# Merging the two halves of each expert chunk into one PSUM bank and one operation, and a reworked weight preparation and load order, in a top-k attention and two-expert kernel

## The chip, the cores and the metric

The kernel runs on one core of a Trainium2 chip. The metric is the device time of one execution in microseconds (us). The five engines are PE (TensorE, with its weight loads shown apart as PEld), DVE (VectorE), ACT (ScalarE), POOL (GpSimd) and SP (SyncE, which here issues every transfer).

## The reference

```python
def _attn_ref(q, k, v):                      # 4 batches, 8 heads, 576 positions, 64 wide
    scores = scale * np.matmul(q, k.transpose(0, 1, 3, 2))
    kth = np.partition(scores, -32, axis=-1)[..., -32:-31]
    scores = np.where(scores >= kth, scores, -1000000000.0)
    scores = scores - np.max(scores, axis=-1, keepdims=True)
    attn = np.exp(scores)
    attn = attn / (np.sum(attn, axis=-1, keepdims=True) + 1e-09)
    return np.matmul(attn, v)

def _moe_ref(x, w_in, w_out):                # 2304 tokens, 512 -> 2048 -> 512
    h = np.maximum(x @ w_in, 0.0)
    return h * h @ w_out

def _moe2_ref(x, w1, w2, w3, w_out):         # 512 -> 768 -> 512
    h = np.maximum(np.maximum(x @ w1, x @ w2), x @ w3)
    return h @ w_out
```

The result is `_moe2_ref(_moe_ref(attention))`, with the attention output laid out as 2304 tokens of 512. Everything is float32 on the outside.

## The kernel before

**Work.** There are 20 attention tiles (four of 128 rows and one of 64 in each of 4 batches), each with 8 heads, and nine expert blocks of 256 tokens, each fed by two or three of the tiles (`BLOCKS`).

**Attention** (`attend`). For one head of one tile PE makes 128x576 scores in two halves (L421), ACT copies them out (L447), and DVE finds the 32nd largest score by four MAX8 passes (L453) with three MATCH_REPLACE8 passes between them (L455). ACT masks and exponentiates (L310, L461, L464), POOL splits off the low half of the exponentials (L307), SP transposes them by DMA (L469), and PE multiplies by the values (L477). When the heads of a tile are done it is normalized, transposed on PE (L506) and written as a pair of float16 tiles, high and low part, into `xt` (L511, L307).

**Expert products.** A float32 product is made of three float16 products (high by high, high by low, low by high), in `group` (L645). The first expert (`moe1`) takes its 2048 hidden columns in 8 chunks of 256, each chunk in two halves of 128: 12 matmuls into one PSUM bank `b`, then ACT's relu with scale (L676), square (L678) and cast (L679), POOL's low part `hl` (L307), and then the second-stage matmuls into the bank pair `a`. A sum of squares per block (L688 on ACT, four small matmuls L694 on PE) gives the scale `ga` with which ACT and DVE write the next expert's input `yt` (L705, L707). The second expert (`moe2`) does the same with three matrices and a running maximum (L723, L726, L730), and its last products go to the output (L758, then SP).

**Weights** (`convert`). The weights come as 64-bit containers in 56 half chunks of 512 KB (L531). In each container the high 32-bit word holds sign and exponent bits to be shifted by three, and the top three bits of the low word are to be filled in below: ACT rescales the high word (L310), DVE shifts the high word left by three (L536) and the low word right by 29 (L534), and POOL adds the two into the float32 weight `w` (L538). PE takes the weights' Gram matrix (L545) for a scale. Then ACT writes the float16 high part (L572), PE makes the remainder as `di` times `w` minus the high part (L579, L580), and ACT copies that out as the low part (L582). Input weights go back to a DRAM scratch and are streamed again for every block (L636); output weights stay in SBUF as `wo` and `wo2`. Conversions of 28 chunks are spread over the first blocks by `feed`; after the second tile of the first block `feed(33)` asks for a share of the rest.

**What sets the order.** All of it is recorded as operations of a `Plan`, which runs a list scheduler over a model of costs (`run`). Each engine's queue is the order that this yields; the program at run time keeps that order and waits on semaphores. Numbers such as `WAIT`, `LW`, `rank`, `slack` and the costs (`c_act`, `c_dve`, `c_pool`, `hop`) act on nothing but the order. Buffers are counted in `nbufs`; among them two for q (`qt`), and six one-bank PSUM buffers `b`. DVE operations with `lock=True` are placed by the planner so as not to overlap POOL operations in its model.

## Time and profile before

| | |
|---|---|
| median of 3 runs | 1054.8 us (1053.51 to 1056.78) |
| profiled execution | 1051.32 us, of which the profiled span is 1049.5 us |
| PE busy | 993.9 us, 95% of the span |
| DVE busy | 847.0 us |
| ACT busy | 824.9 us |
| POOL busy | 659.8 us |
| bytes moved by DMA | 189.46 MB |

How to read it: the profile is one execution, so sums are made against its own 1051.32 us, 1.8 us of which lie outside the span. A busy share near 100% in a stretch says that the engine sets the pace there only if the others wait for it in that stretch. The stretches differ: the first 171.4 us hold attention for the first block and most of the weight preparation and no expert product, the stretch up to 900 us holds attention and expert products side by side, and the rest is expert products alone. Queues are read from rows of instructions in order of time with, in square brackets, the idle time before them and what ended it.

### The profile page before, as it was taken

What the parts mean: (1) busy time and instruction counts of PE and PEld (TensorE: products, weight loads), DVE (VectorE), ACT (ScalarE), POOL (GpSimd) and SP (SyncE); (2) the same over time, 40 slices, a digit from 0 to 9 for tenths busy, and PEclk for the clock granted to TensorE, in tenths of its full rate; (3) what the DMA queues carried; (4) which work ended last, traced back from release to release, by engine and by line L of the source; (5) the groups of instructions that cost most, each with busy time, mean ns of one, the idle gap of its engine ahead of it and who ended that gap; (6) DMA issues with size and microseconds to landing.
All of it is one profiled execution on the core that took longest, in us unless ns stands there. A gap on an engine that the chain in (4) does not pass through costs nothing.

```text
span 1049.5 us, 23814 instructions
## 1 busy us (share of the span) xinstructions
PE 993.9 (95%) x8408; PEld 793.9 (76%) x8408; DVE 847.0 (81%) x1961; ACT 824.9 (79%) x1900; POOL 659.8 (63%) x1126
## 2 busy tenths in 40 slices
PE   4868599999999999999999999999999999999998
PEld 3434346677878787889788889978887888887876
DVE  5999979999895899999999999989999996012011
ACT  4889579999988797998999789989997995452531
POOL 3678656688876566788777667887766765221211
PEclk9978659999999999999999999999999999999999
DMA  9678859988789769678866966875768669335211
GB/s 296 204 204 205 232 125 241 217 199 235 214 222 288 176 138 231 156 173 226 218 166 136 237 149 165 208 207 153 159 173 201 153 130 230 109 100 172 71 44 59
DMA packets 220536, 189.46 MB, mean 181 GB/s; under 512 B 176384, under 2 KB 185344, under 8 KB 220416
## 3 DMA queue, kind: packets, MB, share of 16 engines
q1 hardware_dynamic: 220416, 187.93, 70.3%
q8 instruction: 66, 1.08, 0.4%
q14 instruction: 54, 0.44, 0.1%
HBM read 131.79 MB, written 13.63 MB: 139 GB/s over the span
## 4 chain that ended last, share of the span: by engine, by line
PE 65%; DVE 13%; ACT 7%; DMA 6%; POOL 5%; issue 3%; SPq 0%; POOLq 0%; ACTq 0%; DVEq 0%
PE b L645 35%; PE a L645 12%; PE b L421 8%; DVE mx L453 5%; PE b L477 5%; DVE w L455 5%; PE b L579 3%; DMA wu<-in_w_dram 2%; DMA qs<-in_q_dram 1%; POOL e L307 1%; POOL hl L307 1%; DVE wu L536 1%; DMA qt<-in_q_dram 1%; PE b L545 1%; ACT e L461 1%
## 5 line engine op out<-in xcount | busy, mean ns | idle before, releaser
L453 DVE MAX8 mx<-w 128x8 f32<-128x576 f32 x432 | 315.0, 752 | 0.7
L307 POOL TENSOR_TENSOR e<-e,e 128x512 f16<-128x512 f32 (+1 forms) x288 | 210.1, 741 | 62.9 <-ACT e L464 59.4
L645 PE MATMUL b<-yt,wu 128*128 128x256 f16 x1944 | 227.0, 274 | 3.2 <-ACT r L676 1.0
L645 PE MATMUL b<-xt,wt 128*128 128x256 f16 x1728 | 220.3, 273 | 0.4 <-DVE xt L307 0.4
L645 PE MATMUL a<-hh,wo 128*128 128x256 f16 x1152 | 219.7, 273 | 0.0
L455 DVE MATCH_REPLACE8 w<-mx,w 128x576 f32<-128x576 f32 x288 | 214.1, 746 | 0.0
L645 PEld LDWEIGHTS <-wu 128*128 128x128 f16 x1944 | 186.9, 98 | 29.8 <-issue 4.1
L645 PEld LDWEIGHTS <-wo 128*128 128x128 f16 x1728 | 164.4, 98 | 25.0 <-issue 3.5
L645 PEld LDWEIGHTS <-wt 128*128 128x128 f16 x1728 | 164.7, 98 | 23.8 <-issue 3.1
L307 POOL TENSOR_TENSOR hl<-r,hh 128x256 f16<-128x256 f32 x144 | 97.3, 677 | 106.9 <-ACT hh L679 97.7
L421 PE MATMUL b<-kt,qt 128*128 128x288 f32 (+1 forms) x640 | 157.3, 372 | 6.8 <-DMA qt<-in_q_dram 3.3
L645 PE MATMUL a<-hl,wo 128*128 128x256 f16 x576 | 157.0, 273 | 0.4 <-POOL hl L307 0.4
L421 PEld LDWEIGHTS b<-kt,qt 128*128 128x128 f32 (+1 forms) x640 | 103.2, 201 | 31.8 <-issue 4.1
L310 ACT ACTIVATE e<-s,mx 128x576 f32<-128x576 f32 x144 | 112.3, 781 | 18.3 <-DVE mx L453 16.4
L447 ACT ACTIVATE s<-b 128x288 f32<-128x288 f32 x288 | 108.9, 411 | 14.1 <-PE b L421 13.5
L453 DVE MAX8 mx<-s 128x8 f32<-128x576 f32 x144 | 107.4, 752 | 12.4 <-ACT s L447 12.3
L461 ACT ACTIVATE e<-e,nb 128x576 f32<-128x576 f32 x144 | 112.3, 782 | 4.6 <-POOL nb L457 3.7
L477 PEld LDWEIGHTS <-et 128*128 128x128 f16 (+1 forms) x1440 | 84.6, 102 | 34.3 <-DMA et<-e 14.6
L455 DVE MATCH_REPLACE8 w<-mx,s 128x576 f32<-128x576 f32 x144 | 107.3, 747 | 0.0
L477 PE MATMUL b<-vt,et 128*128 128x129 f16 (+3 forms) x1440 | 93.4, 213 | 13.2 <-ACT s L447 5.2
L464 ACT CAST e<-e 128x576 f16<-128x576 f32 x144 | 97.6, 678 | 0.5
L676 ACT ACTIVATE r<-b,u 128x256 f32<-128x256 f32 x144 | 68.3, 477 | 36.7 <-PE b L645 35.8
(108 smaller groups left out, 1383.6 us busy)
## 6 DMA issues: line engine op xcount, KB each, us to landing
wu<-wsc SPq DMA_DIRECT2D x81, 512.0 KB, 4.2
wt<-wsc SPq DMA_DIRECT2D x72, 512.0 KB, 3.7
wu<-in_w_dram SPq DMA_DIRECT2D x56, 512.0 KB, 5.2
wsc<-oc SPq DMA_DIRECT2D x17, 512.0 KB, 4.8
ks<-in_k_dram SPq DMA_DIRECT2D x12, 576.0 KB, 4.7
qs<-in_q_dram SPq DMA_DIRECT2D x48, 128.0 KB, 3.5
vst<-in_v_dram SPq DMA_DIRECT2D x16, 320.0 KB, 4.3
out_dram<-ot SPq DMA_DIRECT2D x16, 256.0 KB, 2.4
```

What stands on the lines that cost most here:

```text
L307: eng.tensor_tensor(out_ap, a, b, op=ALU.subtract)
L310: return nc.scalar.activation(out_ap, src, AF.Prelu, alpha=slope, **kw)
L421: nc.tensor.matmul(ps[:, 0:HS], a, c, start=m == 0, stop=m == len(seq) - 1)
L447: act(A_S, HS, [ps], [(s, f)], lambda s=s, cs=cs, ps=ps: nc.scalar.activation(s[:, cs], ps[:, 0:HS], AF.Copy, scale=escale))
L453: dve(A_X, S, [src], [(mx, r)], lambda src=src, mx=mx, m8=m8: nc.vector.max(out=mx[:, m8], in_=src[:]))
L455: dve(A_X, S + 50, [src, (mx, r)], [w_], lambda src=src, mx=mx, m8=m8, w_=w_: nc.vector.match_replace(out=w_[:], in_to_replace=mx[:, m8], ...
L461: act(A_E, S, [e, nb], [e], lambda nb=nb, e=e: nc.scalar.activation(e[:], e[:], AF.Exp, bias=nb[:], scale=-1.0 / KEEP), psum=False, ptr=1)
L464: act(A_E, S, [e], [(e16, 0)], lambda e=e, e16=e16: nc.scalar.copy(e16[:, S:2 * S], e[:]), psum=False)
L477: nc.tensor.matmul(ps[0:n, 0:wv], et[:, mm_, c0:c1], vt[:, hh, vc, 0:wv], start=x == 0, stop=x == 8)
L579: nc.tensor.matmul(pl[:], di[:], w[:, cs], start=True, stop=False)
L645: nc.tensor.matmul(o, x, y, start=first and i == 0 and m == 0, stop=last and i == n - 1 and m == 2)
L676: act(MA, N, [ps, u1], [r], lambda r=r, ps=ps, c=c: nc.scalar.activation(r[:, 0:N], ps[:, 0:N], AF.Relu, scale=u1[:, c // 2:c // 2 + 1]), ...
```

## The change

- **Expert chunks.** The two halves of a chunk go into one bank `b` of 128x2x256 (start flag on the first half only), and each of the operations behind them (relu, square, cast, low part; copy, maximum, cast, low part; square with sum, scale, low part of `yt`) is done once over 512 columns instead of twice over 256. `DEEP`, counted in pairs now, goes from 2 to 1, and the counts of the hidden buffers are halved with the tiles twice as wide. The sum of squares needs one small matmul instead of four and one DVE reduce more.
- **Weight preparation.** POOL makes the low three bits from the top byte of the low word (multiply, add, rounded into an integer), and DVE shifts and ors in one operation with two inputs (`scalar_tensor_tensor`). POOL now stands before DVE, not behind it. Every third pair of chunks is held in a `yt` buffer.
- **Remainders of wo2.** For chunks from 25 on (the three of the last matrix) the low part is made by DVE (`DLO = 25`), not by PE and ACT. The GpSimd branch (`PLO = 28`) is never taken, since the last chunk is 27; the tiles `zg, zs, u0, fz` and the branches on `0 == 1` do nothing.
- **Loads and order.** The first k and q loads get a rank of -9; q has three buffers instead of two; the planner reckons 210 ns from a transfer's end to its reader, 1500 ns for reuse of a load's buffer, and a smaller `WAIT`, with other ranks and slacks. The output tile shares the buffers `m`.

```diff
-WAIT = 100.0
+WAIT = 30.0
+MS = 1500.0
+MD = 210.0
+MT = ('qt', 'qs', 'kt', 'ks', 'vst')
...
-                t = max(t, d.end + hop(d.eng, o.eng))
+                t = max(t, d.end + (MD if d.eng == SP else hop(d.eng, o.eng)))
...
-                        t = max(t, sorted(free[k])[u][0] + HOP)
+                        t = max(t, sorted(free[k])[u][0] + (MS if e == SP and b.tag in MT else HOP))
...
-    nbufs = {"ks": 1, "qs": 1, "vst": 1, "kt": 4, "qt": 2, "vt": 4, "sm": 2, "sc": 6, "s": 5, "w": 2, "e": 2, "e16": 3,
+    nbufs = {"ks": 1, "qs": 1, "vst": 1, "kt": 4, "qt": 3, "vt": 4, "sm": 2, "sc": 6, "s": 4, "w": 2, "e": 2, "e16": 3,
...
-             "hh": 4, "hl": 4, "h2": 6, "h3": 6, "r": 3, "m": 2, "ot": 2, ...
+             "hh": 2, "hl": 2, "h2": 3, "h3": 3, "r": 2, "m": 2, ...
...
+            if not kv:
+                plan.rank = -9.0
             if new:
                 kt = prep_k(b, p)
             qt = prep_q(b, t, p)
+            plan.rank = base
...
-                dve(C_D, 512, [hk], [hk], lambda hi=hi: nc.vector.tensor_scalar(
-                    hi().bitcast(U32), hi().bitcast(U32), 3, None, op0=SHL), rate=0.5, slack=SL / 2, lock=True)
-                dve(C_D, 512, [lk], [lk], lambda lo=lo: nc.vector.tensor_scalar(
-                    lo(), lo(), 29, None, op0=SHR), rate=0.5, slack=SL / 2, lock=True)
-                gps(C_P, 445, [hk, lk], [(w, y)], lambda w=w, cs=cs, hi=hi, lo=lo: nc.gpsimd.tensor_tensor(
-                    w[:, cs].bitcast(U32), hi().bitcast(U32), lo(), op=ALU.add))
+                top = lambda raw=raw: raw[:].rearrange("p n u -> p (n u)").bitcast(U8).rearrange("p (n u) -> p n u", u=8)[:, :, 3]
+                gps(C_P, 300, [lk], [lk], lambda lo=lo, top=top: nc.gpsimd.tensor_scalar(
+                    lo(), top(), 1.0 / 32.0, -15.5 / 32.0, op0=ALU.mult, op1=ALU.add))
+                dve(C_D, 512, [hk, lk], [(w, y)], lambda w=w, cs=cs, hi=hi, lo=lo: nc.vector.scalar_tensor_tensor(
+                    w[:, cs].bitcast(U32), hi().bitcast(U32), 3, lo(), op0=SHL, op1=OR), slack=SL / 2, lock=True)
...
+            if chunks[0] >= DLO:
+                for y in range(2):
+                    cs = slice(512 * y, 512 * y + 512)
+                    dve(C_D, 512, [w, ok, sk], [ok], lambda cs=cs, half=half, w=w: nc.vector.scalar_tensor_tensor(
+                        half(1)[:, cs], w[:, cs], sv(), half(0)[:, cs], op0=ALU.mult, op1=ALU.subtract), slack=SL / 2, lock=True)
...
         for c in range(NA):
             wk, w = stream(c, "wt")
+            ps = buf("b", [P, 2, NW])
+            r = buf("r", [P, 2, NW])
             for ff in range(2):
-                ps = buf("b", [P, 512])
-                r = buf("r", [P, NW])
-                group(ps, KD, N, lambda i, wk=wk: [wk, x], lambda kk, w=w, ff=ff: (
-                    cols(w(), 256, kk, ff), (x[:, 0, kk, 0:N], x[:, 1, kk, 0:N])), also=[r])
-                hh, hl = buf("hh", [P, NW], F16), buf("hl", [P, NW], F16)
-                act(MA, N, [ps, u1], [r], lambda r=r, ps=ps, c=c: nc.scalar.activation(
-                    r[:, 0:N], ps[:, 0:N], AF.Relu, scale=u1[:, c // 2:c // 2 + 1]), ptr=1)
...
+                group((ps, ff), KD, N, lambda i, wk=wk: [wk, x], lambda kk, w=w, ff=ff: (
+                    cols(w(), 256, kk, ff), (x[:, 0, kk, 0:N], x[:, 1, kk, 0:N])),
+                    first=ff == 0, last=ff == 1, also=[ps, r])
+            hh, hl = buf("hh", [P, 2, NW], F16), buf("hl", [P, 2, NW], F16)
+            act(MA, 2 * N, [ps, (uu, c // 2)], [r], lambda r=r, ps=ps, c=c: nc.scalar.activation(
+                r[:, :, 0:N], ps[:, :, 0:N], AF.Relu, scale=uu[:, c // 2:c // 2 + 1]), ptr=1)
+            act(MA, 2 * N, [r], [r], lambda r=r: nc.scalar.activation(r[:, :, 0:N], r[:, :, 0:N], AF.Square), psum=False)
+            act(MA, 2 * N, [r], [hh], lambda r=r, hh=hh: nc.scalar.copy(hh[:, :, 0:N], r[:, :, 0:N]), psum=False)
+            gps(A_S, 2 * N, [r, hh], [hl], lambda r=r, hh=hh, hl=hl: sub(nc.gpsimd, hl[:, :, 0:N], r[:, :, 0:N], hh[:, :, 0:N]))
...
-        pe(A_S, 812.0, [yq], [ps, ga], total)
-        dve(A_S, 1, [ps], [ga], lambda: bits(ga[:], ps[:, 0:1], EXP, EXP, AND, XOR))
+        pe(A_S, 200.0, [yq], [ps, ga], lambda: nc.tensor.matmul(ps[:, 0:2], down_t[:], yq[:], start=True, stop=True))
+        dve(A_S, 2, [ps], [ga], lambda: nc.vector.tensor_reduce(ga[:], ps[:, 0:2], op=ALU.add, axis=mybir.AxisListType.X))
+        dve(A_S, 1, [ga], [ga], lambda: bits(ga[:], ga[:], EXP, EXP, AND, XOR))
```

The start of SP's queue is the first place where the order moves. In the rows, `wu` is a half chunk of raw weights, `kt`, `qt` and `vst` are the k, q and v of the first heads; before:

```order
L849 UNCONDITIONAL_BRANCH
L531 DMA wu_124<-in_w_dram 128x1024
L531 DMA wu_132<-in_w_dram 128x1024
L531 DMA wu_134<-in_w_dram 128x1024
L531 DMA wu_136<-in_w_dram 128x1024
L531 DMA wu_138<-in_w_dram 128x1024
L358 DMA kt_140<-in_k_dram 64x1152
L358 DMA qt_143<-in_q_dram 64x256
```

And now:

```order
L548 DMA wu_128<-in_w_dram 128x1024
L548 DMA wu_136<-in_w_dram 128x1024
L548 DMA wu_138<-in_w_dram 128x1024
L368 DMA kt_140<-in_k_dram 64x1152
L368 DMA qt_142<-in_q_dram 64x256
L548 DMA wu_144<-in_w_dram 128x1024
L548 DMA wu_148<-in_w_dram 128x1024
L368 DMA vst_150<-in_v_dram 128x640
```

The first k and q stand behind three half chunks of weights, where they stood behind five.

The start of DVE's queue shows the weight preparation beside the first top-k passes; before (`s` are scores, `mx` the found maxima):

```order
L534 TENSOR_SCALAR wu_136<-wu_136 128x512
L534 TENSOR_SCALAR wu_138<-wu_138 128x512
L536 TENSOR_SCALAR wu_138<-wu_138 128x512
L453 MAX mx_210<-s_190 128x8
L455 MATCH_REPLACE w_215<-mx_210,s_190 128x576
L536 TENSOR_SCALAR wu_166<-wu_166 128x512
L453 MAX mx_210<-w_215 128x8
L534 TENSOR_SCALAR wu_166<-wu_166 128x512
```

And now, where a half chunk is one row that writes the finished weight (`wt`):

```order
L554 SCALAR_TENSOR_TENSOR wt_156<-wu_128 128x512
L554 SCALAR_TENSOR_TENSOR wt_156<-wu_136 128x512
L554 SCALAR_TENSOR_TENSOR wt_174<-wu_138 128x512
L469 MAX mx_204<-s_183 128x8
L554 SCALAR_TENSOR_TENSOR wt_174<-wu_144 128x512
L554 SCALAR_TENSOR_TENSOR wt_216<-wu_148 128x512
L471 MATCH_REPLACE w_224<-mx_204,s_183 128x576
```

Ten DVE rows of the first five half chunks became five, and the first MAX stands behind three of them. Up to the second write of the first block's `xt`, DVE's queue had 288 rows and has 240.

At the end of the last block, ACT's queue before (`r` is a hidden half, `a` the second stage's sums, `yq` their squares):

```order
L676 ACTIVATE r_16259<-b_16258,u_88 128x256
L678 ACTIVATE r_16259<-r_16259 128x256
L679 CAST hh_16288<-r_16259 128x256
L688 ACTIVATE junk,yq_16313<-a_15849 128x256 x2
L688 ACTIVATE junk,yq_16313<-a_15857 128x256 x2
```

And now:

```order
L714 ACTIVATE r_15263<-b_15262,u_88 128x512
L716 ACTIVATE r_15263<-r_15263 128x512
L717 CAST hh_15308<-r_15263 128x512
L726 ACTIVATE junk,yq_15339<-a_14949 128x512
L726 ACTIVATE junk,yq_15339<-a_14958 128x512
```

The last three operations on the hidden columns now cover the whole chunk. On PE the order of the last block is now 24 second-stage matmuls, 24 of the first stage, and so on in turn, and at the end 48 of the second stage, where it was 12 and 12 in turn with 36 at the end.

## Rows read from the trace of the kernel before

**Rows 1.** The page's part 1: busy us, share of the span, instructions.

```profile
PE 993.9 (95%) x8408; PEld 793.9 (76%) x8408; DVE 847.0 (81%) x1961; ACT 824.9 (79%) x1900; POOL 659.8 (63%) x1126
```

**Rows 2.** Busy by stretch: us and count per engine, PE clock, DMA share, GB/s.

```profile
0.00:171.40 171.40, 128.87 (x562) 72.22 (x563) 148.23 (x355) 130.73 (x250) 108.57 (x167) 0.82 0.80 215
171.40:300.00 128.60, 125.67 (x1017) 93.30 (x1015) 119.69 (x280) 117.73 (x263) 97.76 (x155) 1.00 0.83 213
300.00:900.00 600.00, 595.75 (x5617) 507.80 (x5616) 563.24 (x1291) 519.58 (x1252) 424.44 (x757) 1.00 0.77 186
900.00:1049.50 149.50, 143.61 (x1223) 120.57 (x1220) 15.86 (x38) 56.88 (x138) 29.04 (x47) 0.99 0.28 92
```

**Rows 3.** The chain that ended last, by line, of 0 to 60 and 60 to 172 us.

```profile
by line: PE b L421 20.2%; DMA qt<-in_q_dram 14.9%; DVE w L455 10.9%; DVE mx L453 10.1%; issue 7.7%; PE b L579 6.8%; DMA wu<-in_w_dram 6.1%; SPq L531 3.9%; PE b L545 3.0%; PE b L551 2.6%; DVE wu L536 2.6%; DVE wu L534 2.4%; POOL wt L538 1.7%
...
by line: PE b L421 14.8%; PE b L579 11.8%; DVE mx L453 9.6%; issue 8.6%; DVE w L455 8.5%; DMA wu<-in_w_dram 4.8%; PE b L545 4.8%; PE b L477 4.3%; DVE wu L536 4.2%; DVE wu L534 3.4%; ACT wo L572 2.9%; POOL wt L538 2.7%; PE b L580 2.5%; ACT e
```

**Rows 4.** Start of the timeline: start, us, engine, line, instructions, idle before and releaser.

```profile
0.72 2.53 SPq L531 DMA_DIRECT2D wu<-in_w_dram  x5
3.92 0.60 SPq L358 DMA_DIRECT2D qt<-in_q_dram  x1
12.99 8.01 PE L421 MATMUL b<-kt,qt 64*128 64x288 f32 x16 [3.34 <-DMA qt<-in_q_dram]
```

**Rows 5.** Busy by stretch, three stretches of 26 us in the start.

```profile
0.00:26.00 26.00, 12.41 (x45) 8.53 (x46) 14.15 (x32) 12.76 (x24) 8.88 (x22) 1.00 0.94 294
105.00:131.00 26.00, 15.17 (x79) 9.14 (x79) 26.00 (x56) 15.38 (x26) 18.03 (x26) 0.70 0.88 233
131.00:157.00 26.00, 23.69 (x72) 12.27 (x71) 19.89 (x50) 18.54 (x35) 12.82 (x24) 0.50 0.50 123
```

**Rows 6.** Groups by line and shape: busy us, mean ns, idle before and releasers.

```profile
L453 DVE MAX8 mx<-w 128x8 f32<-128x576 f32 x432 | 315.0, 752 | 0.7
L538 POOL TENSOR_TENSOR wt<-wu 128x512 uint32<-128x512 uint32 x32 | 37.6, 1188 | 18.7 <-DVE wu L534 7.5 <-DMA wu<-in_w_dram 4.1 <-PE b L579 3.6
L536 DVE TENSOR_SCALAR wu<-wu 128x512 uint32<-128x512 uint32 x56 | 30.2, 551 | 5.2 <-DMA wu<-in_w_dram 5.0
L534 DVE TENSOR_SCALAR wu<-wu 128x512 uint32<-128x512 uint32 x56 | 27.4, 493 | 4.3 <-ACT wu L310 3.8 <-issue 0.3
L500 POOL TENSOR_SCALAR xg<-xg,va 128x512 f32<-128x512 f32 x16 | 11.4, 713 | 9.3 <-DVE ia L313 6.9 <-DVE va L313 1.8 <-ACT wo L582 0.3
L307 DVE TENSOR_TENSOR xt<-b,xt 128x512 f16<-128x512 f32 x16 | 10.9, 683 | 2.7 <-ACT xt L511 2.7
```

**Rows 7.** One line's instructions: shortest, median, longest ns, first and last start.

```profile
L536 DVE TENSOR_SCALAR wu<-wu x56: 409/424/1331, 4.8 to 300.8; 128x512 uint32<-128x512 uint32 x56
```

**Rows 8.** What SP waited for, 0 to 171 us: us, times, longest.

```profile
SPq L358 <- PE b L421: 18.5, 6, 8.0
```

**Rows 9.** Timeline of PE: one pair of remainders, and the next row.

```profile
173.08 1.02 PE L579 MATMUL b<-wu,di 128*128 128x512 f32 x2
...
174.16 1.47 PE L645 MATMUL b<-xt,wt 128*128 128x256 f16 x12
```

**Rows 10.** Timeline of PE: a block's sum of squares, and the next row.

```profile
567.44 0.95 PE L694 MATMUL b<-yq,down 128*128 128x1 f32 x8
568.25 1.47 PE L645 MATMUL b<-xt,wt 128*128 128x256 f16 x12
```

**Rows 11.** Timeline of the last block: the last hidden half, and the second stage's weight loads.

```profile
1004.63 3.92 PEld L645 LDWEIGHTS <-wo 128*128 128x128 f16 x36
1005.00 0.47 ACT L676 ACTIVATE r<-b,u 128x256 f32<-128x256 f32 x1 [1.26 <-PE b L645]
1006.49 0.67 POOL L307 TENSOR_TENSOR hl<-r,hh 128x256 f16<-128x256 f32 x1 [1.95 <-issue]
```

**Rows 12.** Groups by line and shape, of operations over 512 columns on ACT and POOL.

```profile
L307 POOL TENSOR_TENSOR e<-e,e 128x512 f16<-128x512 f32 x144 | 168.8, 1173 | 62.9 <-ACT e L464 59.4 <-POOL e L307 1.2 <-ACT sc L386 0.8
L758 ACT ACTIVATE ot<-b,go 128x512 f32<-128x512 f32 x18 | 12.3, 682 | 22.1 <-PE b L645 22.0
```

More of the change, by code (lines that the diff above doesn't have):

```diff
@@ L658, in moe1 @@
         av = lambda d: pair[d // 2][:, d % 2, 0:N]
-        def stage2(f, hh, hl):
-            for d in range(KD):
-                also = [(pair[d // 2], 0)] if f in (0, 2 * NA - 1) and d % 2 else []
-                group(acc[d], 1, N, lambda i, also=also: [(wo, f // 2), hh, hl, *also], lambda i, d=d: (
-                    cols(wo[:, f // 2], DM, f % 2, d), (hh[:, 0:N], hl[:, 0:N])),
-                    first=f == 0 and d % 2 == 0, last=f == 2 * NA - 1 and d % 2 == 1)
+        uu = u0 if 0 == 1 and g == 0 else u1
@@ new lines, in stage2 @@
+        def stage2(c, hh, hl):
+            if uu is u0 and c and c % 2 == 0:
+                for pr in pair:
+                    z = slice(c // 2, c // 2 + 1)
+                    act(MA, 2 * N, [pr, (fz, c // 2)], [pr], lambda pr=pr, z=z: nc.scalar.activation(
+                        pr[:, :, 0:N], pr[:, :, 0:N], AF.Copy, scale=fz[:, z]), ptr=1)
+            for ff in range(2):
+                f = 2 * c + ff
+                for d in range(KD):
+                    also = [(pair[d // 2], 0)] if f in (0, 2 * NA - 1) and d % 2 else []
+                    group(acc[d], 1, N, lambda i, also=also: [(wo, c), hh, hl, *also], lambda i, d=d, ff=ff: (
+                        cols(wo[:, c], DM, ff, d), (hh[:, ff, 0:N], hl[:, ff, 0:N])),
+                        first=f == 0 and d % 2 == 0, last=f == 2 * NA - 1 and d % 2 == 1)
@@ L685, in moe1 @@
             stage2(*x_)
-        yq, ga, gx = buf("yq", [P, KD]), buf("ga", [P, 1]), buf("gg", [P, 1])
-        for d in range(KD):
-            act(MA, N, [pair[d // 2]], [(yq, d)], lambda d=d: nc.scalar.activation(
-                junk[:, 0:N], av(d), AF.Square, scale=2.0 ** -27, accum_out=yq[:, d:d + 1]), ptr=1)
+        yq, ga, gx = buf("yq", [P, 2]), buf("ga", [P, 1]), buf("gg", [P, 1])
+        for j, pr in enumerate(pair):
+            act(MA, 2 * N, [pr], [(yq, j)], lambda j=j, pr=pr: nc.scalar.activation(
+                junk[:, 0:2 * N].rearrange("p (a n) -> p a n", a=2), pr[:, :, 0:N], AF.Square, scale=2.0 ** -27, accum_out=yq[:, j:j + 1]), ptr=1)
@@ L690, in moe1 @@
         ps = buf("b", [P, 512])
[L692 to L696 removed]
+        ps = buf("b", [P, 512])
+        pe(A_S, 200.0, [yq], [ps, ga], lambda: nc.tensor.matmul(ps[:, 0:2], down_t[:], yq[:], start=True, stop=True))
+        dve(A_S, 2, [ps], [ga], lambda: nc.vector.tensor_reduce(ga[:], ps[:, 0:2], op=ALU.add, axis=mybir.AxisListType.X))
@@ L713, in moe2 @@
         for fp in range(NF2):
-            m = [buf("m", [P, NW]) for _ in range(2)]
+            m = buf("m", [P, 2, NW])
+            mv = lambda m=m: m[:, :, 0:N]
             kx = lambda fp=fp: u2[:, fp:fp + 1]
@@ L770 @@
         plan.rank = -1.0
-        if g == 0:
+        if g == 0 and 0 == 0:
             feed(33)
```

116 lines of the change are left out of this document (64 added, 52 removed).

## The prediction

> **What bounds the kernel now.** I read the page's busy line first [rows 1]: PE is busy 993.9 us of a span of 1049.5, DVE 847.0. An average over the span says little here, so the second view is the busy time by stretch [rows 2], and it splits the kernel in two. From 171.4 us on, where the first expert matmul starts, PE has 125.67 of 128.6, 595.75 of 600 and 143.61 of 149.5 us: 865.0 of 878.1, 13 us idle. There PE alone sets the pace; what ACT, DVE and POOL save there is worth nothing unless PE waited for it. Before 171.4 us no expert product runs, PE is busy 128.87 us at a mean granted clock of 0.82, and DVE 148.23 us. The third view is the chain that ended last in that start [rows 3]: it changes hands between PE (scores L421, remainders L579), DVE (top-k L453 and L455, and the two weight shifts L536 and L534), POOL's add L538, and transfers. So the start is a mesh in which DVE is the fullest engine but not always the last. The end is then the start's length plus PE's remaining work plus its idle time, and I price the change in these three.
>
> **1. PE's work after the start.** (a) The six wo2 remainders leave PE. One takes from 173.08 to 174.16, 1.08 us [rows 9]: 6.5 us. They were the last of 56 and lay in stretches in which PE is 98% busy. In their place DVE gets six operations of about 0.68 us (L307 on DVE [rows 6]), 4 us before DVE runs out of attention work; the last stretch of rows 2 has DVE at 15.86 of 149.5, so it is hidden by PE's expert work. (b) The sum of squares needed 8 rows of PE from 567.44 to 568.25, 0.81 us [rows 10]; one matmul of two rows leaves 0.2. Eight of nine blocks have them amid other PE work: 8 x 0.6 = 4.9 us. (c) By the order of both kernels, four score matmuls and nine value matmuls that stood ahead of the first expert matmul now stand behind it. Sixteen rows, 8 score matmuls, took 8.01 us [rows 4] at 1.2 GHz, so 0.5 us each at 2.4 GHz: 2.0, with the value ones some 2.5 us added. (d) All expert matmuls are the same in number and width. Net -8.9 us.
>
> **2. PE's idle time after the start.** Merging halves makes each operation on the hidden columns 512 wide. ACT's 512 column row is 682 ns against 470 for 256 [rows 11, 12], 0.21 more in each of three operations; POOL's is 1173 against 670, 0.50 more. That saves some 45 us of ACT over the kernel, which I count as nothing: PE's expert matmuls cover it. But the chain from the last hidden half to its low part was 1005.00 to 1007.16 [rows 11] and becomes 1.1 us longer, to 1008.3. In the order now, 24 first-stage matmuls and 24 second-stage ones lie between, at 3.92 / 36 = 0.109 us each [rows 11] 5.2 us, more than the chain of 3.7 us from 1004.63. So only the very last chunk shows: 24 second-stage matmuls cover 2.6 us, to 1007.25, and PE then waits 1.0 us for its chunk. Next, the squares, the sum and the new `yt` are two wide operations in place of four, with a reduce more: half a us either way, taken as 0. The tail after the last output matmul does not change. Net +1.0 us.
>
> **3. The start.** Three edits act on it. *First loads:* the score matmuls began at 12.99 after waiting for q, which was issued at 3.92 behind five weight loads [rows 4]. Two of these now come after it: 1.05 MB at 294 GB/s [rows 5] is 3.5 us. *DVE:* 39 half chunks stand ahead of the second `xt` write in both orders. Each cost 551 + 493 = 1.04 us [rows 6]. The new form does not occur before. The nearest row is a two-input operation over 512 columns, L307 on DVE at 683 ns [rows 6]; alone, the two old ones are 0.42 each [rows 7], so the new one saves 0.16 without contention and 0.36 if contention stays with the old. 39 x 0.36 = 14 us at best, 6 at worst short of a loss (rival E). DVE's queue also holds four MAX8 and three MATCH_REPLACE8 fewer ahead of that write, some 5 us at 752 ns [rows 6]. *POOL:* the add of 1188 ns becomes a one-input operation; the nearest row is L500's 713 ns [rows 6]. If everything on DVE counted, the start would shrink by 14 + 5 + 3.5 = 22 us. Counting what the chain held instead [rows 3]: the shifts have 5.0% of 60 us and 7.6% of 112, 11.5 us, of which a third goes, 3.8; POOL's add 4.0 us, of which 0.4 goes, 1.6; with the loads 9 us. I take 12, nearer to the chain, because DMA (0.80 of 171.4 us) and ACT (130.73) are close behind DVE in rows 2 and their work is the same. The third q buffer goes with this: SP waited 18.5 us for scores to release q, 8.0 at once [rows 8], and everything behind a waiting load on SP, weights and transposes, waited too. I give it no own price; it is what would let the 12 us come about.
>
> **Sum.** 1051.3 - 12 - 8.9 + 1.0 = 1031.4 us, 19.9 below the profiled execution. That execution is 3.5 us under the median of the runs, 1054.8, so for the median 1035 us.
>
> **The rivals.** *B, PE's clock holds.* From 105 to 157 us the granted clock was 0.70 and then 0.50 [rows 5], which is 1.2 GHz of 2.4, after a stretch in which PE was busy 15.17 of 26 us; in the second it was busy 23.69 of 26. With the higher level the same work takes half, 12 us less: 1023. For it: PE's remainders and score matmuls are spread more evenly in the new order, and the shifts that held up Gram matmuls are shorter. Against: DVE still sets the pace, so PE will still pause.
>
> *C, another engine takes over the start.* DMA needs 0.80 x 171.4 = 137 us of work and ACT 131; with queues in order and hops between, 160 us may be out of reach. Then only the loads show, or nothing: 1043.5 to 1047. For it: the shares in rows 2; against: DMA itself waited, with a share of 0.50 from 131 to 157 [rows 5].
>
> *D, no change.* The 9 us taken from PE come back as idle time, since PE's queue is in order and coarser expert operations hold banks longer, and the start stands: 1055. Against: 4 us of idle in 600 [rows 2] leave few waits to grow.
>
> *E, slower, by contention between DVE and POOL.* The shift's median is 424 ns and its longest 1331 [rows 7], 0.9 us more, as if it waited for most of one POOL operation of 1.04 to 1.19 us. The Trainium skill (SBUF — State Buffer, "Who interferes with whom") says that a DVE instruction with two SBUF inputs and a POOL instruction that reads SBUF exclude each other for the whole instruction; by that rule the new operation is exposed as the old ones were, and the longest row agrees with it. In this kernel that would mean: each new operation, 0.68 us, waits for one whole POOL operation, 1.17 [rows 12], 1.85 us against 1.04, 39 times: +31.5 us, less 5 and 3.5, +23 on the start: 1055 + 23 - 8 = 1070. It decides from 39 x (x - 1.04) = 16.4 (5, 3.5 and the 7.9 net of parts 1 and 2), a mean of x = 1.46 us per new operation. Against: the old pair, exposed twice, averaged only 0.2 us of it, and one instruction is exposed once.
>
> **Chances and range.** The forecast (1026 to 1043) 0.45, B 0.20, C 0.18, D 0.07, E 0.10. A measurement here tells some 0.3%, 3 us, from no change. A, B and C are faster, 0.83; D the same, 0.07; E slower, 0.10. The range runs from 1017, into B, to 1054, to the edge of D; beyond lie about 0.05 and 0.14.
>
> **What would show it.** Right: the first expert matmul near 159 us; first score matmul near 9.5; the new DVE operation at 0.65 to 0.8 us and POOL's at about 0.7; no remainder of wo2 on PE; PE still at 98% or more from the first expert matmul on, with about 1 us of wait before the last second-stage chunk. Wrong: the first expert matmul at 168 us or later (C, or E where the new DVE operation is above 1.3 us), or under 150 with the clock at 1.0 throughout (B), or PE idle clearly above 14 us after it (D). The largest risk is the 12 us, taken between 9 and 22, where one stall of transfers or one stretch at the lower clock is worth as much as the whole term.

## The result, and the profile after

The changed kernel takes 1025.2 us (median of 4, 1021.8 to 1027.4) against 1054.2 (1052.6 to 1056.8) of the kernel before on the same chip: a ratio of 0.972, with an interval of 0.968 to 0.976. The forecast was 1035 with a range of 1017 to 1054: the direction and the range held, and the gain is 29 us where 20 were forecast. The profiled execution took 1023.4 us, 28.0 less than before's.

The page's first part, busy time and share of each engine, answers to [rows 1]:

```profile
PE 969.9 (95%) x8336; PEld 779.5 (76%) x8336; DVE 824.0 (81%) x1848; ACT 773.5 (76%) x1570; POOL 628.6 (62%) x1027
```

PE lost 24.0 us of busy time, and the rest of its span fell from 55.6 to 51.7 us. That is the shortest account of the result: 24 us less busy, 4 us less idle. Not all of the 24 is work taken away; some 7.6 us of it are the clock, as worked out under the control for scatter below. ACT has 51 us less to do, and nothing in these two numbers needs it.

Busy time by stretch, split at the first expert matmul as in [rows 2] (us and count for PE, PEld, DVE, ACT, POOL, then PE's granted clock, DMA share, GB/s):

```profile
0.00:149.90 149.90, 117.56 (x547) 64.81 (x548) 131.70 (x301) 125.52 (x240) 94.75 (x162) 0.90 0.86 246
149.90:300.00 150.10, 142.65 (x1204) 111.87 (x1204) 143.99 (x329) 137.67 (x273) 115.98 (x181) 0.98 0.84 215
300.00:872.00 572.00, 567.81 (x5384) 484.33 (x5382) 535.20 (x1196) 467.71 (x989) 393.15 (x659) 1.00 0.77 187
872.00:1021.60 149.60, 141.90 (x1208) 118.46 (x1206) 13.06 (x24) 42.61 (x70) 24.73 (x26) 0.99 0.27 90
```

The first expert matmul comes at 149.9 us instead of 171.4, 21.6 earlier. In the start PE's idle time fell from 42.5 to 32.3 us; behind it the idle time rose from 13.1 to 19.3, and of these 6.2 us the stretch up to 300 us has 4.5. The other half of the 21.6 is PE's busy time: 547 matmuls stand ahead of the marker for 562, which is some 2 us, and the rest is the clock (0.90 for 0.82 in these rows, which leave out the first 43 us; see below).

The start of the timeline answers to [rows 4] (start, duration, engine and line, operation):

```profile
2.75 0.63 SPq L368 DMA_DIRECT2D qt<-in_q_dram  x1
3.42 1.07 SPq L548 DMA_DIRECT2D wu<-in_w_dram  x2
...
9.91 4.17 PE L431 MATMUL b<-kt,qt 64*128 64x288 f32 x8 [1.85 <-DMA qt<-in_q_dram]
```

q is issued 1.2 us earlier, two weight loads behind it, and the scores begin 3.1 us earlier, for 3.5 in the working. The new operations, by line (duration in ns as min/median/max), answer to [rows 6, 7]; first DVE's, then POOL's, then DVE's remainder of wo2:

```profile
L554 DVE SCALAR_TENSOR_TENSOR wt<-wu x24: 672/683/1052, 5.5 to 113.1; 128x512 uint32<-128x512 uint32 x24
L554 DVE SCALAR_TENSOR_TENSOR wu<-wu x24: 671/684/1031, 113.7 to 294.8; 128x512 uint32<-128x512 uint32 x24
L554 DVE SCALAR_TENSOR_TENSOR yt<-wu x8: 673/680/1242, 30.7 to 85.1; 128x512 uint32<-128x512 uint32 x8
```

```profile
L552 POOL TENSOR_SCALAR wu<-wu x56: 639/657/706, 4.8 to 292.7; 128x512 uint32<-128x512 uint8 x56
```

```profile
L592 DVE SCALAR_TENSOR_TENSOR wo<-wu,v,wo x6: 733/742/910, 165.6 to 307.9; 128x512 f16<-128x512 f32 x6
```

They cost what the nearest rows said. Contention between DVE and POOL shows little on DVE: the longest, 1242 ns, is 0.57 us over the shortest. It shows on POOL. In the timeline, one small operation on POOL undisturbed, and the same operation beside a run of five new ones on DVE (the fifth writes `yt`, from 71.80 to 72.48):

```profile
98.09 0.30 POOL L474 TENSOR_SCALAR nb<-mx 128x1 f32<-128x1 f32 x1
...
69.40 2.48 DVE L554 SCALAR_TENSOR_TENSOR wt<-wu 128x512 uint32<-128x512 uint32 x4
69.59 3.06 POOL L474 TENSOR_SCALAR nb<-mx 128x1 f32<-128x1 f32 x1 [0.85 <-DVE mx L469]
```

It ends at 72.65, behind the whole run. Against the median of their kind, fifteen POOL operations beside the new ones lost 15.2 us in all, and the new ones 1.5. In the kernel before, reckoned alike, POOL lost 11.2 us beside the two shifts and the shifts 11.0. So DVE's gain is in part contention that it no longer pays, while POOL pays more; what that costs the whole kernel no run separates.

Two views by line show what left PE. First before (busy us, mean ns of one, idle ahead), lines that were not among the rows above:

```profile
L421 PE MATMUL b<-kt,qt 128*128 128x288 f32 (+1 forms) x640 | 157.3, 372 | 6.8 <-DMA qt<-in_q_dram 3.3 <-ACT oc L582 1.5 <-ACT xs L480 1.5
...
L579 PE MATMUL b<-wu,di 128*128 128x512 f32 x48 | 25.3, 609 | 0.6 <-ACT oc L582 0.6
...
L694 PE MATMUL b<-yq,down 128*128 128x1 f32 x72 | 9.3, 245 | 0.4
L580 PE MATMUL b<-wo,nid 128*128 128x512 f16 x22 | 8.6, 391 | 0.0
```

and the same lines after:

```profile
L431 PE MATMUL b<-kt,qt 128*128 128x288 f32 (+1 forms) x640 | 148.8, 362 | 7.5 <-POOL qt L310 3.4 <-DMA qt<-in_q_dram 1.8 <-ACT xs L497 0.8
...
L605 PE MATMUL b<-wu,di 128*128 128x512 f32 x36 | 18.9, 607 | 0.2 <-POOL di L578 0.2
...
L606 PE MATMUL b<-wo,nid 128*128 128x512 f16 x16 | 6.6, 411 | 0.0
...
L731 PE MATMUL b<-yq,down 128*128 128x2 f32 x18 | 3.0, 238 | 2.3 <-ACT junk L726 2.3
```

The six remainders account for 6.4 + 2.0 = 8.4 us, the sums of squares for 6.3. The same 640 score matmuls take 8.5 us less, though nothing in them changed; the lower clock makes part of it. Matmuls of different groups overlap on PE, and a group's busy time counts the overlap too, so such differences don't add up to the 24.0 and come out larger than the time that they free.

### The profile page after: what moved, and what is told of

The parts are those of the page before. It is cut to its first block, busy times and chain, and to the rows that moved or that the text cites. A ratio compares the mean times of both kernels' runs of the same rounds, so it can differ in the third digit from the quotient of the medians.

```text
span 1021.6 us, 23034 instructions
## 1 busy us (share of the span) xinstructions
PE 969.9 (95%) x8336; PEld 779.5 (76%) x8336; DVE 824.0 (81%) x1848; ACT 773.5 (76%) x1570; POOL 628.6 (62%) x1027
## 4 chain that ended last, share of the span: by engine, by line
PE 61%; DVE 19%; ACT 7%; DMA 6%; POOL 5%; issue 3%; SPq 0%; POOLq 0%; ACTq 0%; DVEq 0%
PE b L671 34%; PE a L671 10%; DVE mx L469 9%; DVE w L471 8%; PE b L431 7%; PE b L494 4%; PE b L605 3%; DMA wsc<-oc 2%; DMA vst<-in_v_dram 1%; DMA wu<-in_w_dram 1%; POOL e L310 1%; DMA et<-e 1%; DMA qt<-in_q_dram 1%; POOL kt L310 1%; ACT e L313 1%
## 5 line engine op out<-in xcount | busy, mean ns | idle before, releaser
L469 DVE MAX8 mx<-w 128x8 f32<-128x576 f32 x432 | 311.2, 746 | 0.4
L671 PE MATMUL b<-xt,wt 128*128 128x256 f16 x1728 | 213.2, 273 | 0.0
L671 PE MATMUL a<-hh,wo 128*128 128x256 f16 x1152 | 209.8, 273 | 0.0
L431 PE MATMUL b<-kt,qt 128*128 128x288 f32 (+1 forms) x640 | 148.8, 362 | 7.5 <-POOL qt L310 3.4
L310 POOL TENSOR_TENSOR hl<-r,hh 128x512 f16<-128x512 f32 x72 | 84.5, 1174 | 88.5 <-ACT hh L717 86.5
L431 PEld LDWEIGHTS b<-kt,qt 128*128 128x128 f32 (+1 forms) x640 | 100.8, 198 | 38.2 <-issue 10.5
L313 ACT ACTIVATE e<-s,mx 128x576 f32<-128x576 f32 x144 | 112.1, 778 | 19.9 <-DVE mx L469 17.7
L463 ACT ACTIVATE s<-b 128x288 f32<-128x288 f32 x288 | 105.8, 411 | 20.4 <-PE b L431 19.4
L469 DVE MAX8 mx<-s 128x8 f32<-128x576 f32 x144 | 107.1, 746 | 6.7 <-ACT s L463 6.7
L494 PE MATMUL b<-vt,et 128*128 128x129 f16 (+3 forms) x1440 | 91.0, 212 | 3.0 <-POOL vt L310 2.8
L714 ACT ACTIVATE r<-b,u 128x512 f32<-128x512 f32 x72 | 49.6, 689 | 47.4 <-PE b L671 47.0
```

Source lines behind the costliest of these rows:

```text
L310: eng.tensor_tensor(out_ap, a, b, op=ALU.subtract)
L313: return nc.scalar.activation(out_ap, src, AF.Prelu, alpha=slope, **kw)
L431: nc.tensor.matmul(ps[:, 0:HS], a, c, start=m == 0, stop=m == len(seq) - 1)
L463: act(A_S, HS, [ps], [(s, f)], lambda s=s, cs=cs, ps=ps: nc.scalar.activation(s[:, cs], ps[:, 0:HS], AF.Copy, scale=escale))
L469: dve(A_X, S, [src], [(mx, r)], lambda src=src, mx=mx, m8=m8: nc.vector.max(out=mx[:, m8], in_=src[:]))
L494: nc.tensor.matmul(ps[0:n, 0:wv], et[:, mm_, c0:c1], vt[:, hh, vc, 0:wv], start=x == 0, stop=x == 8)
```

## The experiments

Twelve kernels ran. Theory D says that DVE's work sets the length of the start; its rival O that the order of the queues, transfers or the clock set it. Theory P says that what PE no longer does counts in full; its rival I that it comes back as idle time. For the merged halves, C, M and N are told in the expectation. Each kernel is `after` or `before` with one edit. The table has what the profiled execution of each shows: the first expert matmul, PE's busy time, how much of it lay at the lower clock (1.2 GHz; how that was counted stands with the control for scatter), and PE's idle time (span less busy); the ratio is to runs of the kernel before on the same chip.

| kernel | ratio (interval) | first expert matmul | PE busy | of it at the lower clock | PE idle |
|---|---|---|---|---|---|
| before | 1 | 171.4 | 993.9 | 79.3 | 55.6 |
| after | 0.972 (0.968 to 0.976) | 149.9 | 969.9 | 64.1 | 51.7 |
| e1_late_kq | 0.977 (0.972 to 0.982) | 154.1 | 978.0 | 85.3 | 51.8 |
| e2_two_q | 0.978 (0.972 to 0.984) | 154.3 | 974.1 | 76.1 | 58.0 |
| e3_old_prep | 0.984 (0.979 to 0.989) | 154.3 | 972.9 | 69.5 | 62.2 |
| e4_wo2_pe | 0.976 (0.971 to 0.980) | 149.8 | 975.3 | 63.0 | 51.8 |
| e5_old_plan | 0.980 (0.978 to 0.983) | 147.8 | 980.8 | 78.5 | 51.8 |
| e6_halves | 0.975 (0.971 to 0.978) | 149.7 | 973.0 | 73.1 | 50.4 |
| e7_prep_only | 1.004 (1.002 to 1.006) | 159.2 | 991.2 | 69.5 | 61.9 |
| e8_merge_twice | 1.011 (1.008 to 1.014) | 178.7 | 983.4 | 89.8 | 81.5 |
| e9_wait33 | 0.973 (0.968 to 0.977) | 154.7 | 977.4 | 80.4 | 50.8 |
| e10_plan_only | 0.993 (0.990 to 0.996) | 150.3 | 985.9 | 72.5 | 55.7 |
| e11_prep_plan | 0.987 (0.983 to 0.991) | 152.3 | 992.1 | 85.2 | 48.6 |
| e12_short_shl | 0.995 (0.992 to 0.998) | 169.4 | 992.8 | 78.7 | 52.6 |

**One part of `after` undone.** The first k and q load without their rank:

```
-            if not kv:
-                plan.rank = -9.0
```

> The changed kernel (1025.2 us) without the early rank of the first k and q loads. Theory D (DVE's work sets the length of the start, so all that delays its first MAX8 delays the end): the first score matmul moves from 9.9 back to about 13 us and the first expert matmul from 149.9 to about 153; 1028.7 us. Rival O (the start was shortened by the order of loads and buffers and by PE's clock, DVE's time is hidden): the mesh absorbs the 3 us; 1025 us.

Measured: 1029.2 us, first scores at 13.3 us. The idle time is after's; PE's busy time rose by 8, with 21 us more of it at the lower clock. The marker stands 4 us later, but the idle time ahead of it is after's too (31.8 for 32.3 us), and the interval of the ratio overlaps that of `after`: that the early loads are worth anything is not shown.

The third q buffer:

```
-"qt": 3,
+"qt": 2,
```

> The changed kernel with two q buffers instead of three. Theory D: SP waits again for scores to release q, but DVE stays the fullest engine; first expert matmul at 150 to 153 us, 1025 to 1028 us. Rival O: the wait of SP that was 18.5 us in the kernel before comes back, weights and transposes behind it are late; first expert matmul at 158 us or later, 1033 us or more.

Measured: 1030.4 us, PE idle 6.3 us more. This part works through waits, as the prediction thought, and has by the medians a price of its own of some 5 us that was put at nothing; but here too the intervals overlap.

The old weight preparation (two shifts on DVE, the add on POOL, for one DVE operation behind one on POOL) in the new kernel:

```
-                gps(..., nc.gpsimd.tensor_scalar(lo(), top(), 1.0 / 32.0, -15.5 / 32.0, op0=ALU.mult, op1=ALU.add))
-                dve(..., nc.vector.scalar_tensor_tensor(w[:, cs], hi(), 3, lo(), op0=SHL, op1=OR))
+                dve(..., nc.vector.tensor_scalar(hi(), hi(), 3, None, op0=SHL))
+                dve(..., nc.vector.tensor_scalar(lo(), lo(), 29, None, op0=SHR))
+                gps(..., nc.gpsimd.tensor_tensor(w[:, cs], hi(), lo(), op=ALU.add))
```

> The changed kernel with the weight preparation of before: two DVE shifts of some 0.5 us and POOL's add of 1.13 us in place of POOL's 0.66 us and DVE's one operation of 0.70 us. Theory D: 39 half chunks in the start cost 0.33 us of DVE each more, 13 us; first expert matmul at 163 us, 1038 us. Rival O: DVE's time is hidden; first expert matmul at 150 to 154, 1025 to 1030 us.

Measured: 1037.0 us, 12 above `after`. The time is D's, the place is not: the marker moved by 4.4 us only. The stretches:

```profile
0.00:154.30 154.30, 114.80 (x540) 63.93 (x541) 140.26 (x346) 127.20 (x244) 108.13 (x162) 0.87 0.88 239
154.30:1035.10 880.80, 858.11 (x7798) 718.59 (x7796) 692.45 (x1559) 649.10 (x1327) 541.88 (x866) 0.99 0.68 173
```

Ahead of the marker PE idled 39.5 us for 32.3, behind it 22.7 for 19.3, and it had 7 matmuls more left to do there. So a marker hides part of what a change of the start is worth; PE's idle time over the whole span shows it, +10.5. This edit gives back POOL's saving together with DVE's, so it does not tell which of the two the 12 us belong to.

The six remainders of wo2 back on PE:

```
-    DLO = 25
+    DLO = 99
-    PLO = 28
+    PLO = 99
```

> The changed kernel with the six wo2 remainders back on PE (and ACT), none on DVE. Theory P (PE sets the pace after the start, so its work counts in full): 6 x 1.08 = 6.5 us more, 1031.7 us, first expert matmul where it was. Rival I (PE's idle time after the start rose from 13 to 19 us in the changed kernel, so part of the work taken from PE came back as waits): 2 us or less, 1025 to 1027 us.

Measured: 1027.6 us, and in the profiled execution 5.5 us over after's: PE busy +5.4, idle +0.1, at the lower clock as much as in `after`. P's mechanism stands in the trace; the ratio's interval alone would not tell it from `after`.

The old numbers of the planner in the new kernel:

```
-WAIT = 30.0
+WAIT = 100.0
-    AVS = 800.0
+    AVS = 0.0
-    TA = 2.0
+    TA = 0.0
-    C0, C1 = 1.5, 0.03
+    C0, C1 = 0.5, 0.06
```

with the two terms MD and MS taken out. The early rank of the first loads, the third q buffer and everything else of `after` stay.

> The changed kernel, all its operations and buffers, ordered with the planner's numbers of the kernel before (WAIT 100, no own delays for transfers and load buffers, no slack on the value matmuls, ranks and due times as before). Theory D (DVE's and PE's saved work carries the gain): 1025 to 1031 us, first expert matmul at 150 to 156. Rival O (the order carries it): at least half of the start's 21.6 us comes back, first expert matmul at 161 us or later, 1036 us or more.

Measured: 1033.5 us, clearly above `after`, with a marker that is even earlier, 147.8. These numbers are worth 8 to 9 us, and the marker does not show it. PE's busy time is 11 us higher at an unchanged idle time, and 14 us more of it lie at the lower clock.

Separate halves in the expert stages, each half with its bank and its operations, with everything else as in `after`:

```
-            ps = buf("b", [P, 2, NW])
-            r = buf("r", [P, 2, NW])
             for ff in range(2):
+                ps = buf("b", [P, 512])
+                r = buf("r", [P, NW])
...
-    DEEP = 1
+    DEEP = 2
```

> The changed kernel with the first and second expert's chunks in halves again, one bank and one set of operations each, as before (the sum of squares and the writing of yt stay merged). Theory C (merging is hidden by PE's expert matmuls, as ACT's 45 us less were counted at nothing): within 3 us of 1025. Rival M (the longer chain of wide operations makes the 6 us of idle time that PE gained after the start): idle after the first expert matmul falls from 19 to 13 us, 1019 us. Second rival N (ACT's and DVE's saved time matters in the crowded stretch up to 300 us): 5 us or more slower, 1030 us.

Measured: 1026.3 us; idle 50.4 against 51.7. C holds: the part that gives the change its name makes no difference that can be measured, and the 38 us of ACT that it saves (811.3 for 773.5 busy) were all covered.

**More of the new operation.** `after` with each of the 56 new DVE operations issued twice in place, the order of all queues unchanged:

```
+                    for _ in range(2):
                         nc.vector.scalar_tensor_tensor(...)
```

> The changed kernel with each shift-and-or on DVE issued twice (56 more operations of 0.68 us, 39 of them in the start), with the order of all queues otherwise unchanged. Theory D: 39 x 0.68 = 27 us on the start, first expert matmul at 175 us, 1050 us. Rival O (DVE is not what the others wait for): 10 us or less, 1035 us. If DVE is the last to arrive in about half of the start, some 13 us, 1038 us.

Measured: 1066.1 us, 41 above `after`. The start (same columns as above):

```profile
0.00:178.70 178.70, 126.26 (x547) 68.90 (x548) 168.52 (x345) 127.65 (x243) 94.17 (x165) 0.85 0.75 209
```

DVE has 36.8 us more there, the marker moved by 28.8, near D's 27, and PE's idle time ahead of it rose by 20.1. Over the span DVE has 53.7 us more and PE idled 29.8 more, so more than half of the work added to DVE came through as waits of PE; most of what the 41 us hold beyond that goes with the lower clock (89.8 us of PE's busy time for 64.1). The mean of the operation rose to 0.81 to 0.87 us by tile.

**Less DVE work at an unchanged order.** `before` with the left shift on 64 of its 512 columns; all queues stay as they are:

```
-                    hi().bitcast(U32), hi().bitcast(U32), 3, None, op0=SHL)
+                    hi().bitcast(U32)[:, 0:64], hi().bitcast(U32)[:, 0:64], 3, None, op0=SHL)
```

> Before with the left shift of each prepared half chunk on 64 of its 512 columns (the other columns keep unshifted values, so the output is not the reference's); every queue has the same instructions in the same order. The shift takes some 0.1 us for 0.51, 39 of them ahead of the first expert matmul: 16 us less on DVE. Theory D (DVE sets the start's length): first expert matmul at 155 to 160 for 171.4. Rival O (order, transfers or the clock set it): within 3 us of 171.4. For the whole time: 1040 if PE keeps what the start gains, 1050 to 1055 if it is given back behind the first expert matmul, as with the new preparation alone.

Measured: 1046.9 us, marker at 169.4. The left shift is L534, the one that waits for ACT, and the right shift L536; the description of the kernel before has the two lines the other way round. The left shift took 189 ns (median) for 421, and DVE's busy time in the start fell by 8.0 us, half of what was expected; 2 us reached the marker. D fails here at the marker. What happened instead, in POOL's waits for the two shifts, first before, 0 to 171.4 us (total, times, longest):

```profile
POOL wt L538 <- DVE wu L534: 7.5, 4, 6.4
POOL wu L538 <- DVE wu L536: 5.2, 5, 2.5
POOL wt L538 <- DVE wu L536: 3.5, 4, 1.2
```

and with the short shift, 0 to 169.4 us:

```profile
POOL wt L538 <- DVE wu L534: 12.9, 4, 8.0
POOL wt L538 <- DVE wu L536: 2.3, 3, 0.9
```

The waits fell by 1 us only, 16.2 to 15.2, and those for the shorter shift grew: what is late is mostly the turn of a shift in DVE's queue, not its length. Over the span DVE has 12.3 us less, PE idled 3.0 us less, and the median is 4.8 us lower (2 to 8 by the interval). So in an order that was made for the longer work, work taken from DVE came through less than work added: a quarter of it in PE's idle time, where it was more than half in the kernel with the doubled operation.

**Preparation and order apart.** `before` with the new preparation alone (the edit of e3 the other way round):

> The kernel before with only the new weight preparation (POOL's low bits, DVE's one shift-and-or). Theory D: 39 half chunks in the start at 0.33 us less of DVE each, 13 us; 0.988 of the kernel before, first expert matmul near 160 us. Rival O: nothing, 0.997 to 1.003.

Measured: 1057.4 us. The marker fell by 12.2 us, as D said, and the time still rose. In the waits of POOL and SP over the whole span (total, times, longest):

```profile
POOL wu L535 <- DMA wu<-in_w_dram: 39.5, 29, 6.3
```

```profile
SPq L469 <- POOL wu L535: 22.4, 7, 3.8
```

POOL's new operation is now the first of its chain beside ACT's to need a weight load, and it stands ahead of attention work: POOL waited 39.5 us there, and the transposes that SP issues (L469) waited for POOL. In `after` the first wait is less than half:

```profile
POOL wu L552 <- DMA wu<-in_w_dram: 17.1, 15, 3.5
```

Behind its marker e7 idled 22.2 us for 13.1, more than any gain: its idle time over the span is 61.9 for 55.6. That these waits make the loss is read from the rows and not tested; the old planner numbers alone do not bring them, since e5 has the same numbers and preparation and 21.4 us of the first wait.

Then `before` with the order alone: planner numbers, ranks, first loads and the third q buffer of `after`, and the old preparation:

```
-WAIT = 100.0
+WAIT = 30.0
+MS = 1500.0
+MD = 210.0
...
-"qt": 2, ... "s": 5
+"qt": 3, ... "s": 4
...
+            if not kv:
+                plan.rank = -9.0
```

> Before with the new planner numbers, ranks, first loads of k and q and the third q buffer, but the old weight preparation, separate halves and wo2 remainders on PE. Theory A (the parts add up): after with wo2's remainders back on PE would be about 1031, the new preparation without these numbers was 1057, so they are worth 26 us; before less 26 is 1028, ratio 0.975. Rival S (order and preparation only pay together, since the numbers were fitted to the new preparation): 1048 to 1058, ratio 0.995 to 1.004.

Measured: 1044.4 us for 1051.7 of before on that chip. A's 1028 is out; S's range is missed by 4 us. The marker is the surprise:

```profile
0.00:150.30 150.30, 112.06 (x517) 62.99 (x518) 135.81 (x338) 123.28 (x237) 98.55 (x158) 0.89 0.83 223
```

It stands at 150.3, where after's is, with the old operations and hardly a gain. PE did 517 matmuls ahead of it for 562, and its idle time over the span is before's, 55.7: the order put expert work earlier and left other work for later.

And both together, with separate halves, four squares and the remainders on PE as in `before` (the edits of e7 and e10 in one kernel):

> The new preparation alone (1057 us, first expert matmul at 159) with the new planner numbers, ranks, first loads and third q buffer added; separate halves, four squares and wo2's remainders on PE as in before. Both theories: after's 1025 and 5.5 for the remainders on PE, 1031, ratio 0.978, first expert matmul near 150, PE idle behind it 18 to 22 us. If it stays above 1040, merging the halves or the squares matters after all, against what separate halves alone showed (1026).

Measured: 1040.1 us, idle 48.6. Alone the two gave 1.004 and 0.993, in product 0.9975; together 0.987. So S holds in its mechanism: some 1% comes only from having both. PE's idle time says it more plainly: +6.3 and +0.1 us alone, -7.0 together. The 1031 of the expectation is missed by 9 us. This kernel differs from e6 by the remainders, the sums of squares, the writing of `yt` in four pieces for two and a few buffers, and takes 13 us more; by PE's lines the first have 9.3 us of it, and the sum of squares, 3.0 in e6, is

```profile
L704 PE MATMUL b<-yq,down 128*128 128x1 f32 x72 | 9.4, 243 | 0.5
```

6.4 more; without the overlap that lines count, the prediction's rows give 6.5 and 4.9, 11.4 of the 13. The expectation counted 5.5 for the first and nothing for the second.

**A control for scatter.** `after` with WAIT at 33, which shuffles the order a little:

> After with one planner number changed (WAIT 33 for 30), so that the same instructions come in a slightly different order. It shows how much the time scatters by order alone. Theory R (the differences of 4 to 9 us that one edit made so far have their causes in that edit): within 3 us of after, 1022 to 1028. Rival L (any other order lands several us off, whatever its reason): off by 5 us or more, and then differences of that size say nothing of one edit.

Measured: 1023.2 us: R holds for the median. But the four executions went from 1022.2 to 1030.0, and the profiled one is the longest:

```profile
PE 977.4 (95%) x8336; PEld 784.0 (76%) x8336; DVE 823.7 (80%) x1848; ACT 775.4 (75%) x1570; POOL 632.8 (62%) x1027
```

Its idle time is 0.9 us below after's and its busy time 7.5 above, for the same instructions. The clock tells why. The record of the granted clock begins late, 43.4 us into the span of `before`, 42.5 in `after`, 27.9 in e6, and the means of a stretch count what lies ahead of it as 1.00. But score matmuls there take as long as where 0.50, that is 1.2 GHz, is on record. First `before` from 122 to 159 us, on record at 0.50, and from 28 to 42, ahead of the record (shortest, median, longest ns); then `after` (no record yet) and e6 (record begun, at 1.00) from 28 to 34:

```profile
L421 PE MATMUL b<-kt,qt x24: 681/684/846, 130.3 to 154.9; 64*128 64x288 f32 x24
L421 PE MATMUL b<-kt,qt x12: 684/684/846, 28.3 to 39.6; 64*128 64x288 f32 x12
L431 PE MATMUL b<-kt,qt x4: 684/685/847, 30.2 to 31.8; 64*128 64x288 f32 x4
L431 PE MATMUL b<-kt,qt x7: 402/403/657, 27.4 to 30.6; 64*128 64x288 f32 x7
```

In all fourteen kernels the score matmuls ahead of the record are the long ones. The table's column counts that time as lower clock, together with the stretches on record at 0.50. Eight of the kernels have after's PE work: `after`, e1, e2, e3, e5, e6, e8 and e9. Their busy times spread over 13.5 us, 969.9 to 983.4; less half of what lay at the lower clock they lie between 935.4 and 941.6, and without e5 within 3.1 us. So I take half of that time as what the lower clock cost (an estimate; the score matmuls, 402 ns of 684, would say 0.41), and the rest as PE's work. By it the 7.5 us of the control and the 8 us of e1 are the clock's, and 7 of e5's 11. The control's idle time hardly moved, so the differences of 6 us and more in it (e2, e3, e7, e8) are probably of another kind; one control is no measure of scatter.

## Why the prediction was right, and where not

**PE's work: right in its terms, with a part that it does not have.** Terms (a) and (b) said 6.5 and 4.9 us. Undoing (a) alone gave PE 5.4 us of busy time, 6.0 without the clock, and 5.5 of time in the profiled execution. That the lines show 8.4 and 6.3 is the way they count: a remainder has some 1.4 us by the lines of the kernel before (25.3 / 24 + 8.6 / 22) and 1.08 from start to start [rows 9]. The prediction's rival D, that this comes back as idle time (theory I of the runs), finds no support in e4, with 0.1 us of idle time, though the medians alone would not rule it out. The charge (c) of 2.5 us for work moved behind the marker holds too, with 15 matmuls and some 1.9 us. But PE's work over the span fell by 16.4 us (954.2 to 937.8, the clock taken out), not 11.4. The other 5 go with the order: e10 and e11, with the new order and the old PE work, have 949.6 and 949.5, e7 and e12, without the new order, 956.5 and 953.4. What in the order makes them is open.

**PE's idle time behind the marker: the step that failed.** It said +1.0 and was +6.2. The place that it named was right: the chunk of the last block, in the timeline of after,

```profile
974.88 0.69 ACT L714 ACTIVATE r<-b,u 128x512 f32<-128x512 f32 x1 [3.24 <-PE b L671]
...
978.21 0.27 PE L671 MATMUL a<-hl,wo 128*128 128x256 f16 x1 [0.70 <-POOL hl L310]
```

has a chain of 3.3 us (3.7 in the working) and a wait of 0.7 (1.0), which answers to [rows 11]. But this wait is a small part. The working had put the rest of PE's idle time there at no change, since the kernel before waits so little there, and 4.5 of the 6.2 us lie between the marker and 300 us, where preparation and attention run beside the first expert blocks. PE's waits there, in after, begin with (total, times, longest)

```profile
PE b L431 <- POOL qt L310: 3.4, 2, 3.2
```

where before had none above 1.1. The 3.2 us among them end at 243.35, while the first block's squares and its `yt` are under way and PE has no expert matmul to put in. POOL's timeline just ahead of it:

```profile
239.59 1.16 POOL L310 TENSOR_TENSOR e<-e,e 128x512 f16<-128x512 f32 x1
...
241.46 0.65 POOL L552 TENSOR_SCALAR wu<-wu 128x512 uint32<-128x512 uint8 x1
242.20 0.30 POOL L474 TENSOR_SCALAR nb<-mx 128x1 f32<-128x1 f32 x1
242.58 0.72 POOL L310 TENSOR_TENSOR qt<-qs,qt 128x256 fp32r<-128x256 f32 x1
```

The q tile waits its turn behind attention's other operations and the weights' bits: POOL, on average the emptiest of the compute engines, is late here. One operation shortly before, at 234.63, had taken 2.08 us for 0.30 beside a run of new operations on DVE. This is one execution's picture, not a shown cause: e6 idled 18.6 us behind its marker with hardly any such wait, and an early marker by itself does not bring the idle time, since e11, with its marker at 152.3, idled 14.8 there. What all of the 6.2 us come from stays open.

**The start: the 12 us came, and the clock on top.** 12 us were taken of a possible 22, and the marker moved by 21.6. Of these 10.2 are idle time, some 1.9 the moved matmuls, together the 12; the other 9.5 are the lower clock, with 56.8 us of PE's busy time there for 75.9, which the prediction had as rival B and not in its sum. The parts were sized well: the loads 3.1 us for 3.5; 39 new operations took 25.8 us for 39.7 of the old pairs, 13.9 less, for "14 at best"; the POOL operation 0.66 us for about 0.7. That the 12 was met is partly luck: it was a choice between 9 and 22, and by the runs the order and the preparation together are worth 13 to 14 us of the whole time (e11), while neither part alone is, which the working did not know.

**The sum.** Measured on the profiled executions: start -21.6, idle behind it +6.2, PE's busy time behind it -12.6, together -28.0; the working had -12, +1.0 and -8.9. With the lower clock taken out (-9.5 in the start, +2.0 behind it) the measured terms are -12.1, +6.2 and -14.6, together -20.5, for -19.9 in the working. So the start was right, and two misses of 5 to 6 us with opposite signs cancel, which is luck; the rest of the gain, some 7.6 us, is the clock's.

**The rivals, by the prediction's letters.** *E* is out by its own mark: the new operation's mean is 0.70 to 0.75 us by tile, for a threshold of 1.46. The Trainium skill (SBUF — State Buffer, "Who interferes with whom") says that a DVE instruction with two SBUF inputs contends with a POOL instruction that reads SBUF, for a port pair that is locked to one of them. The rows agree with it, on DVE with 0.57 us in the longest, on POOL with 3.06 us for 0.30. What E had wrong is who waits: it let DVE pay. *C* is out for the marker: transfers ran at a share of 0.86 for 0.80 and did not stop it at 160. *B* came true in part, in the profiled execution. In the stretches of [rows 5] the clock is now

```profile
105.00:131.00 26.00, 21.14 (x125) 12.00 (x123) 25.72 (x63) 24.02 (x48) 20.31 (x36) 0.96 0.78 197
131.00:157.00 26.00, 25.82 (x144) 15.49 (x144) 23.18 (x55) 22.08 (x44) 16.01 (x27) 0.80 0.89 218
```

0.96 and 0.80 for 0.70 and 0.50, and PE is no longer idle for 10.8 of 26 us ahead of it (4.9 now). B said 12 us; over the start it was 9.5, over the span 7.6. Whether the change brings this is not shown: by the table, kernels without the new order have 69.5 to 79.3 us at the lower clock, those made from `after` 63.0 to 89.8, and the control, with after's operations in almost after's order, 80.4.

## What to carry to other kernels

Where one engine carries the end, add up its busy and idle time over the whole span, and take apart how much of the busy time lay at which clock; the instant at which a stage begins can move by 20 us because work was put elsewhere. An operation made cheaper on an engine with a fixed queue order can pay little, or cost, until the order is made for it: try the part and the order alone and together before either is judged. Work taken off an engine that is 98% busy counted here nearly in full (6.0 us of 6.5 in e4's trace), and work taken off its neighbours, here 38 us of ACT, may count for nothing.
